# Windowed attention with an MLP-mixer block: the order of the operations written anew

## The chip, the cores and the metric

The kernel runs on one core of a Trainium2 chip. The engines named below are PE (matrix multiplication; PEld is its load of weights, which overlaps), DVE (elementwise work), ACT (elementwise work and functions such as exp and relu), POOL (here it only issues transfers, on a queue of its own) and SP (issues transfers on another queue). PSUM is the memory in which PE leaves its sums; it has 8 banks. The metric is the time of one execution in microseconds (us) on the device, the median of several runs.

## The reference

```python
scores = q @ k.T / sqrt(D) + bias          # B=8, H=8, S=576, D=64
mask = (rel >= 0) & (rel < 128)            # rel = i - j; bias = -slope[h] * |rel|
attn = exp(where(mask, scores, -1e9) - max); attn /= attn.sum(-1) + 1e-9
x = (attn @ v) with the heads side by side # [8, 576, 512]

h = relu(x.T @ w_tok1) @ w_tok2            # per batch: 512x576 @ 576x256 @ 256x576
u = x + h.T
out = u + relu(u @ w_ch1) @ w_ch2          # 576x512 @ 512x1536 @ 1536x512, f32
```

The kernel works in bfloat16 with sums in float32. It takes exp without subtracting the maximum and gets the sum of a row of attention from a column of ones beside v.

## The kernel before, in words

**Stages of a batch.** Each of the 8 batches goes through the same stages, and in time neighbouring batches are laced into one another, so that the attention of a batch fills in among the channel matmuls of the batch before.

- `load` (line 587, issue at 597): POOL fetches 128 rows of q, k or v for all heads, converted on the way.
- `transposes` (line 736): SP turns a piece of q and k by a DMA (line 744), at the start PE does it (line 755).
- `scores` (line 772): PE multiplies q and k for one block of 128 keys (line 792, 16 matmuls), ACT takes exp (line 807), DVE multiplies by the mask (line 817). `scores_two` (line 825) does two smaller ones.
- `values` (line 855): PE multiplies by v (line 872), DVE takes the reciprocals of the sums (line 902) and divides (line 905); ACT can divide too (line 910).
- `token_mix` (line 916): the two token matmuls (lines 934 and 977), relu between them (line 952), `ub` = x + h (line 995, DVE). u is then turned: by SP (line 1003) or by PE (line 1012) with a copy (line 1018).
- `unit` (line 1361) and `halves` (line 1343): the first channel matmul. In six of the batches it goes in three units each, 18 units in all, where seven products of half-size blocks take the place of eight. `halves` makes the sums of inputs (DVE, line 1355). A product is 4 matmuls on PE (line 1392) into a PSUM bank. `keep` copies a bank to a float32 buffer (ACT, line 1407, or DVE, line 1408), `join` adds a bank to such a buffer (DVE, line 1416), then relu (line 1418 or 1420).
- `second` (line 1605): the second channel matmul, also by seven products (PE, line 1669). `evict` adds a bank and u into an output buffer (DVE, line 1640) and `store` sends it out (line 1652; SP, and POOL in batches 5 and 6).
- The last 64 rows of S are done for a pair of batches at once (lines 1535 and 1580 on PE, 1587 on DVE, 1596 the store).

**Buffers.** Every kind of buffer is a ring of a fixed number of slots: 5 for q with k, 5 for v, 7 for turned q and k, 3 for exp, 6 of 128x512 float32 (`ob`; both `keep` and the output use them), 8 banks of PSUM and others. An operation that takes a slot waits for everything that still uses what was in it, transfers out of it among them.

**The order.** The program first collects 1559 operations, numbered in the order in which they are made; numbers are written in base 36. `follow` (line 132) then reads three strings:

```python
seq = [self.ops[number(x)] for x in ORDER.split()]
for x in ELSEWHERE.split():
    o = ops[number(x)]
    o.eng, o.cost, o.emit = o.other
line = {e: [o for o in seq if o.eng == e] for e in ("PE", "ACT", "DVE", "POOL", "SP")}
places = iter(PLACES)
for o in seq:
    for b in o.bufs:
        if b.slot is None:
            first = number(next(places))
```

`ORDER` holds all numbers once; each engine carries out its own operations in the order in which they stand there, one after the other, so that an operation that waits holds up all behind it on its engine. `ELSEWHERE` names the operations that run on their other engine (ACT for DVE, or DVE for ACT). `PLACES` gives, in the order of first use, the slot of each new buffer. `emit` writes the program out in the order of the planned starts. Which engine an operation waits for follows from the data and from the slots; nothing in the operations themselves depends on the strings.

**Operations that the prediction names**, all of batch 3 and the pair before it unless a batch is given:

| numbers | line | engine | what |
|---|---|---|---|
| dw, dx, dy | 1669, 1640, 1652 | PE, DVE, SP | last product of a second channel matmul, its eviction, the store |
| dm, du, dq, 97, 9j | 1652 | SP | stores of other output buffers |
| dz, e0, e1, e2 | 1580 | PE | three matmuls each of the pair's last rows |
| e3 | 1587 | DVE | the addition behind them, into an `ob` slot |
| gi, gg, gm, gk | 1012 | PE | turns of u, four small matmuls each |
| gs, gw, gz, gu | 1392 | PE | products of a unit |
| h0 | 1407 / 1408 | ACT / DVE | `keep` copy of a product, into an `ob` slot |
| j6 | 792 | PE | a block of scores |
| j5, jb, jy | 744 | SP | turns of q and k |
| sr, t2 | 792, 872 | PE | a block of scores of batch 5, and values of batch 5 |
| 30, 33 | 597 | POOL | loads of v for batch 5 (rows 0 to 127, 128 to 255) |
| 38, 37, 3d, 36 | 597 | POOL | loads of q and k for batches 6 and 7 |

Of the kernel before, what the change touches and what calls it, by code (L numbers as in the profile page):

```python
# [70 lines left out]
class Plan:  # L71
# [60 lines left out]
    def follow(self):  # L132
        def number(x):
            return int(x, 36)

        ops, seq = self.ops, [self.ops[number(x)] for x in ORDER.split()]
        assert sorted(o.n for o in seq) == list(range(len(ops)))
        for x in ELSEWHERE.split():
            o = ops[number(x)]
# [5 lines left out]
        for o in ops:  # L145
            for d in o.deps:
                succ[d].append(o)
        places = iter(PLACES)
        for o in seq:
# [134 lines left out]
    def emit(self, spin):  # L284
# [20 lines left out]
        for _, _, go in sorted(work, key=lambda w: w[:2]):  # L305
# [37 lines left out]
ORDER = ("h i 4z f j g 52 k d e 0 l 59 7 1 2 8 4v m 3 4 4x n 4w 9 4y o a 55 5 41 50 42 56 43 53 57 44 51 p 58 54 5c q "  # L343
# [45 lines left out]
ELSEWHERE = ("4w 4y 56 5m 63 6i 71 74 78 7b 83 88 8q a5 b6 b9 c1 c3 c5 c7 c9 cj ct d3 ez fb fm fo fv g7 gh gt h6 hn i0 jk "  # L389
             "kd kg lj m0 mi mn o3 o5 pa pj pk qe qj rl rq tg ts u1 vg vn wd wi xo xq yv z4 z5 10f 10k 115 11d 12o 13b 13j "  # L390
             "13k 14l 14q 15e 15r 15w")
PLACES = ("003232244671006170016710104526473452324062714260014501022433200524173120165202465372440110001732024053675420"
          "360171042072526432720541210436114220732031100742150456206221031425610041602504206145025061031240402506450223"
          "452311670240535411003123434022130102043060114030654026104631102122032427523422017541020305640072430141305303"
          "616053003220074112200332410054176020041170345022171620132114760274303704202761355326450110130100760053143531"
          "400040251014632204003247206114537242472530264130031205304206723450251006425001454210307106420052457433163102"
          "754002075110427205524235200432307526201035207114713217106024701450404360211500207226702220541062352046021000"
          "013723101045303540003364101470053317212605030540155440361105412")
UNIT_LATE = False
SECOND_LATE = False  # L400
GATE = True
# [1360 lines left out]
```

## Time and profile before

| | |
|---|---|
| median of 3 runs | 273.8 us (273.27 to 274.88) |
| the profiled execution | 274.09 us, span 272.3 us, granted clock 1.00 |
| PE / PEld busy | 262.8 us (96%) / 198.8 us (73%) |
| DVE busy | 240.2 us (88%) |
| ACT busy | 161.6 us (59%) |
| POOL busy (issuing) | 114.8 us (42%) |
| moved by DMA | 38.61 MB, mean 142 GB/s |

The span is the time from the first to the last instruction of the profiled execution; its own time lies 1.8 us above it. A group line gives line, engine, operation, output and inputs, then the count, busy time and mean duration of one, and the idle time ahead of it with what ended that. In the view by stage each engine has its busy time and, in brackets, its count of instructions in that stretch; then the granted clock of PE, the share of the DMA engines and their rate. A row of the chain is start, length, engine and line; a row of the waits says who waited for whom, the total, the count and the longest. In a timeline row the bracket at the end is the idle time just before and what released it.

### The profile page before, as it was taken

To read this page: it belongs to the slowest core of one execution; us is meant where nothing else is said; L and a number is where in the kernel's file an instruction comes from. 1 tells how busy PE (TensorE), PEld (TensorE's weight loads), DVE (VectorE), ACT (ScalarE), POOL (GpSimd) and SP (SyncE) were. 2 spreads that over 40 slices of the span, in tenths; PEclk is the share of its full clock that TensorE was granted. 3 is DMA by queue.
4 is the path that set the end of the run, shared out by engine and by line. 5 is a ranking of instruction groups with operands and counts; after the bars stand their busy time and mean duration, and the time that the engine had idled before them with its cause. 6 is when DMAs were issued, how large, how long until landed. Compare 5 with 4: busy or idle time off the path is not lost.

```text
span 272.3 us, 7636 instructions
## 1 busy us (share of the span) xinstructions
PE 262.8 (96%) x3069; PEld 198.8 (73%) x3069; DVE 240.2 (88%) x553; ACT 161.6 (59%) x314; POOL 114.8 (42%) x147
## 2 busy tenths in 40 slices
PE   7989999999999989999999999999999999999994
PEld 4767566676686667588776877688885878689883
DVE  7886699997997789999999799999999899895993
ACT  6875696335883489509883099418963199505700
POOL 8987986627093092801980181602511220013000
PEclk9999999999999999999999999999999999999999
DMA  8999999999999999999999799988997430045006
GB/s 201 179 159 181 157 195 183 152 168 123 204 186 126 220 125 161 143 141 204 149 143 178 180 162 194 109 94 212 132 128 76 116 99 4 19 80 195 0 2 193
DMA packets 160339, 38.61 MB, mean 142 GB/s; under 512 B 146544, under 2 KB 159472, under 8 KB 160304
## 3 DMA queue, kind: packets, MB, share of 16 engines
q0 software_dynamic: 109968, 19.64, 88.5%
q1 hardware_dynamic: 49104, 17.70, 36.3%
q10 hardware_dynamic: 1232, 0.79, 1.0%
q8 instruction: 24, 0.39, 0.6%
q14 instruction: 11, 0.09, 0.1%
HBM read 35.85 MB, written 9.44 MB: 166 GB/s over the span
## 4 chain that ended last, share of the span: by engine, by line
PE 79%; DMA 9%; DVE 4%; ACT 4%; issue 2%; POOL 1%; DVEq 0%; POOLq 0%; ACTq 0%
PE ps L1669 27%; PE ps L1392 17%; PE ps L1492 7%; PE ps L872 5%; PE ps L977 4%; PE ps L792 4%; PE ps L934 4%; PE ps L1535 4%; PE ps L1580 3%; DMA qk<-in_k_dram 3%; DMA v<-in_v_dram 2%; DMA W<-in_moe_w_tok_dram 2%; ACT pe L807 2%; DMA out_dram<-raw 1%; DVE r L1416 1%
## 5 line engine op out<-in xcount | busy, mean ns | idle before, releaser
L807 ACT ACTIVATE pe<-ps 128x1024 bf16<-128x1024 f32 (+1 forms) x56 | 51.9, 974 | 17.8 <-PE ps L792 17.8
L597 POOL DMA_DIRECT2D qk<-in_k_dram x35 | 30.2, 873 | 42.0 <-DMA qkT<-qk 39.8
L1669 PEld LDWEIGHTS <-r 128*128 128x128 bf16 x384 | 36.6, 98 | 7.5 <-issue 1.7
L597 POOL DMA_DIRECT2D v<-in_v_dram x36 | 31.0, 873 | 23.7 <-PE ps L872 21.7
L597 POOL DMA_DIRECT2D qk<-in_q_dram x35 | 30.2, 875 | 18.5 <-DMA qkT<-qk 15.6
L1407 ACT COPY raw<-ps 128x512 f32<-128x512 f32 x41 | 23.7, 603 | 15.2 <-PE ps L1392 14.0
L1416 DVE TENSOR_TENSOR r<-ps,raw 128x512 bf16<-128x512 f32 x46 | 30.9, 680 | 2.1 <-PE ps L1392 1.3
L1392 PE MATMUL ps<-tt,WS 128*128 128x256 bf16 x216 | 31.0, 273 | 1.4 <-DVE raw L1587 1.4
L1669 PEld LDWEIGHTS <-s 128*128 128x128 bf16 x288 | 27.6, 98 | 6.2 <-DVE s L1517 0.8
L817 DVE TENSOR_TENSOR pe<-pe,mask 128x1024 bf16<-128x1024 bf16 (+1 forms) x48 | 30.5, 646 | 1.6 <-ACT pe L807 1.4
L1392 PEld LDWEIGHTS <-WS 128*128 128x128 bf16 x288 | 26.5, 98 | 6.9 <-issue 2.4
L910 ACT ACTIVATE xb<-ps,rt 128x64 bf16<-128x64 f32 (+1 forms) x88 | 20.4, 331 | 18.4 <-DVE rt L902 18.0
L1669 PE MATMUL ps<-WC,r 128*128 128x256 bf16 x192 | 25.7, 273 | 0.0
L872 PEld LDWEIGHTS <-pe 128*128 128x128 bf16 (+1 forms) x480 | 20.2, 99 | 6.3 <-issue 1.3
L1669 PE MATMUL ps<-WT,s 128*128 128x256 bf16 x192 | 24.8, 273 | 0.0
L1669 PE MATMUL ps<-WT,r 128*128 128x256 bf16 x192 | 24.4, 273 | 0.0
L872 PE MATMUL ps<-v,pe 128*128 128x65 bf16 (+1 forms) x480 | 23.1, 194 | 0.1
L1392 PEld LDWEIGHTS <-WC 128*128 128x128 bf16 x216 | 20.0, 98 | 4.3 <-issue 0.8
L1640 DVE TENSOR_TENSOR raw<-ps,ub 128x512 f32<-128x512 f32 x28 | 19.2, 684 | 4.5 <-PE ps L1669 3.9
L1652 POOL DMA_DIRECT2D out_dram<-raw x8 | 5.7, 720 | 38.5 <-DVE raw L1640 38.1
L995 DVE TENSOR_TENSOR ub<-ps,xb 128x512 bf16<-128x512 f32 x32 | 20.9, 681 | 1.0 <-PE ps L977 1.0
L1392 PE MATMUL ps<-uT,WC 128*128 128x256 bf16 x144 | 20.7, 273 | 0.0
(146 smaller groups left out, 521.1 us busy)
## 6 DMA issues: line engine op xcount, KB each, us to landing
out_dram<-raw SPq DMA_DIRECT2D x20, 256.0 KB, 3.2
qk<-in_q_dram POOLq DMA_DIRECT2D x30, 128.0 KB, 5.3
qk<-in_k_dram POOLq DMA_DIRECT2D x30, 128.0 KB, 5.6
v<-in_v_dram POOLq DMA_DIRECT2D x28, 128.0 KB, 5.2
WC<-in_moe_w_ch_dram POOLq DMA_DIRECT2D x8, 384.0 KB, 7.4
out_dram<-raw POOLq DMA_DIRECT2D x8, 256.0 KB, 2.7
v<-in_v_dram POOLq DMA_DIRECT2D x16, 64.0 KB, 4.6
out_dram<-ob SPq DMA_DIRECT2D x4, 256.0 KB, 3.0
```

Of the source, the lines that this page charges most:

```text
L597: nc.gpsimd.dma_start(out=to()[p0 : p0 + n, :, :], in_=rows(src, b, s0, n))
L807: act_.activation(out=pb()[:, e, :, lo:, c0:c1_], in_=wide(e)[:, :, lo:, c0:c1_], func=ACT.Exp, scale=scale)
L817: dve_.tensor_tensor(out=o, in0=o, in1=heads(mk, es), op=ALU.mult)
L872: pe_.matmul(view(e)[a:z, i, :], lhsT=pb()[:, e, i, kind, a:z], rhs=vb()[:, HEADS[e][i], 0 : D + 1], start=start, stop=stop, skip_group_ch ...
L910: act_.activation(out=x4()[:, i, :], in_=view(e)[r0:r1_, i, 0:D], func=ACT.Copy, scale=rt()[r0:r1_, 0, i, :])
L995: plan.op("DVE", 690, lambda blk=blk, ht=ht, hs=hs: dve_.tensor_tensor(out=ub()[:, blk, :], in0=ht()[:, hs], in1=xb()[:, blk, :], op=ALU.a ...
L1392: pe_.matmul(bk()[:, c * HS : (c + 1) * HS], lhsT=l(c, cb), rhs=r(cb), start=new and c == 0 and cb == 0, stop=cb == 1, skip_group_check=True)
L1407: return plan.op("ACT", 600, lambda: act_.copy(out=e()[:, :], in_=bk()[:, :]), rk + UNIT_RANK, makes=e, uses=[bk], other=("DVE", 690, lamb ...
L1416: add = plan.op("DVE", 690, lambda: dve_.tensor_tensor(out=o(), in0=half_of(bk), in1=half_of(e), op=ALU.add), rk + UNIT_RANK, uses=[bk, e] ...
L1492: pe_.matmul(ct()[:, :], lhsT=WC1[:, cb, t * P : (t + 1) * P], rhs=uT()[:, cb, :], start=cb == 0, stop=cb == NCB - 1)
L1640: dve_.tensor_tensor(out=v, in0=bk().rearrange("p (c n) -> p c n", c=2), in1=src, op=ALU.add)
L1669: pe_.matmul(bk()[:, c * HN : (c + 1) * HN], lhsT=l(t, c), rhs=w(t), start=first, stop=g == 1 and t == HK - 1, skip_group_check=True)
```

## The change

`ORDER`, `ELSEWHERE` and `PLACES` are replaced. The first 129 entries of `ORDER` stay as they were, and nothing else in the file is touched: the same 1559 operations with the same data dependencies, another order on each engine, another choice of slots and banks. `ELSEWHERE` goes from 76 to 71 entries: 35 operations return to their first engine, 30 others move away from theirs. PE, SP and POOL keep their counts (555, 80, 142); ACT goes from 244 to 245, DVE from 538 to 537. The three rows of `ORDER` with the operations of the table, before and after, the whole of `ELSEWHERE` and the start of `PLACES`:

```diff
--- before.py
+++ after.py
@@ -343,59 +343,59 @@
...
-         "dt gb gd g9 gf dw j5 dz dx gi gg gj gm e0 kg gh gn gk jy dm jb du gl go e1 gq j6 gs j9 gp e2 j7 gr gw h9 gt "
-         "dy dq gz e3 gx ha h0 ja gy j8 26 29 2p gu gv jn h4 h1 jq jh h5 jo hb h2 jr jp jj hc h7 h8 hg hd hi he hh jk "
...
-         "nu 2y 3b 32 iz 35 36 sp iv sq pz q3 mz nf q1 33 nb 3a u1 q5 30 n7 n8 q7 q6 px q4 sw nc n0 nh n9 ni nl nj nk "
-         "ng nm nn np nq nr q9 nv qd sr qe qa ss qh qf qg qk qb qi st nw nx qm ql qp su qn t8 t2 sv t4 qc t5 qq qu qj "
...
-ELSEWHERE = ("4w 4y 56 5m 63 6i 71 74 78 7b 83 88 8q a5 b6 b9 c1 c3 c5 c7 c9 cj ct d3 ez fb fm fo fv g7 gh gt h6 hn i0 jk "
-             "kd kg lj m0 mi mn o3 o5 pa pj pk qe qj rl rq tg ts u1 vg vn wd wi xo xq yv z4 z5 10f 10k 115 11d 12o 13b 13j "
-             "13k 14l 14q 15e 15r 15w")
-PLACES = ("003232244671006170016710104526473452324062714260014501022433200524173120165202465372440110001732024053675420"
...
+         "fu d6 fv g1 g2 dr g3 g4 fz fw g0 g5 g6 ds 27 2a 28 do g7 4q dl dt j5 4n 29 2s 2c 2d 26 gc ge dm dp gf ga gb "
+         "g8 97 9j dq du dv dw jb gd g9 2j gm dx dz gn gk gi dy gj gl gg gh go 4r e0 gq j6 gw 4j gp gr gs j7 gt j8 e1 "
+         "gx j9 e2 gu gz e3 gv h9 h0 gy ja ha 9b jn h4 jh 2g 2h jq h5 h1 jo hb h7 hc 2m jj jr h8 h2 jp hg hd he hh hi "
...
+         "m0 ph mt nd mq mu mw ls pi pj pk mb mc sp 30 38 ps lt mx pt mr ms pu n4 mv my sw n5 pv n6 mz q2 py pw ne q3 "
+         "q7 me 37 3d 36 px na sr nt nb pz nf q0 n7 ss st nc q1 su u1 sv n1 nu 33 t2 nh n8 n0 n9 t4 md q4 q5 ni 3e 3j "
...
+ELSEWHERE = ("4w 4y 56 5m 63 6i 6u 74 7b 7m 83 86 88 a5 at b6 b9 bz c5 cf cl cr d1 el en f9 fm ft fw gj gn h0 hn i8 jk jv "
+             "kd kg lm m0 m5 o3 o5 pj pk pu rl rq tg ts ty u1 ux vn wd xo xq yv yx 10f 10k 115 11a 11d 12o 13b 13k 13v 14g "
+             "14t 159")
+PLACES = ("403222140674016170016700104526373452324062704260014501012423400107514612541720056420512131043042027522651042"
+          "007613652044203135257326220570034113040370002746354165011546311124526020421426042021003204035040225665320347"
...
```

On SP the operations around dy stand before as j4, j5, jy, dm, jb, du, dy, dq and after as j4, j5, dm, 97, 9j, dq, du, jb, dy, 9b, jy. On POOL the loads around 30 stand after as 30, 38, 37, 3d, 36, 33.

More of the change, by code (lines that the diff above doesn't have):

```diff
@@ L345 @@
          "x 6v 5u 5r y 6j 5s 46 47 66 72 6k 5v z 6a 48 6b 10 6d 6l 6g 6e 6h 6f 67 6m 6c 68 6i 11 69 6n 6p 6o 12 6s 6q "
[43 rows of a table removed]
-ELSEWHERE = ("4w 4y 56 5m 63 6i 71 74 78 7b 83 88 8q a5 b6 b9 c1 c3 c5 c7 c9 cj ct d3 ez fb fm fo fv g7 gh gt h6 hn i0 jk "
-             "kd kg lj m0 mi mn o3 o5 pa pj pk qe qj rl rq tg ts u1 vg vn wd wi xo xq yv z4 z5 10f 10k 115 11d 12o 13b 13j "
-             "13k 14l 14q 15e 15r 15w")
-PLACES = ("003232244671006170016710104526473452324062714260014501022433200524173120165202465372440110001732024053675420"
[L393 to L398, printed above, removed]
[43 rows of a table added]
+ELSEWHERE = ("4w 4y 56 5m 63 6i 6u 74 7b 7m 83 86 88 a5 at b6 b9 bz c5 cf cl cr d1 el en f9 fm ft fw gj gn h0 hn i8 jk jv "
[3 more added lines that the diff above has]
+          "007613652044203135257326220570034113040370002746354165011546311124526020421426042021003204035040225665320347"
+          "300256411702243512201540323101004320010107502744157602651020002645247315241414207451121212071462333104055231"
+          "171100345060146251130211301004353065612020557002725623107602374440172000674524310300201337300241005361211024"
+          "621325034033016206121743240105764242326240265130404012323675043030454042360520460016224100100751055136120021"
+          "740207504103720553410521413204760332451134000732410207012401634052460012502613420153070520340263420152164327"
+          "013114360320304006750642347000240565720451120053170305025631420")
 UNIT_LATE = False
```

77 rows, old and new, of the table ORDER are left out of this document.

## The prediction

> **What bounds the kernel now.** I read the page's busy shares and chain by engine first, then busy time by stage, then the chain in order of time, last the waits.
>
> ```profile
> PE 262.8 (96%) x3069; PEld 198.8 (73%) x3069; DVE 240.2 (88%) x553; ACT 161.6 (59%) x314; POOL 114.8 (42%) x147
> ...
> PE 79%; DMA 9%; DVE 4%; ACT 4%; issue 2%; POOL 1%; DVEq 0%; POOLq 0%; ACTq 0%
> ```
>
> ```profile
> core 0: us, PE busy (x) PEld busy (x) DVE busy (x) ACT busy (x) POOL busy (x), PEclk, DMA share, GB/s
> 30.00:95.00 65.00, 65.00 (x727) 44.12 (x727) 57.17 (x127) 39.67 (x78) 34.43 (x42) 1.00 1.73 171
> 95.00:113.00 18.00, 16.30 (x207) 12.03 (x206) 16.85 (x43) 16.06 (x33) 12.73 (x16) 1.00 1.56 145
> ...
> 133.00:140.00 7.00, 6.68 (x91) 4.77 (x90) 6.97 (x16) 5.55 (x12) 7.00 (x9) 1.00 2.20 142
> ...
> 140.00:160.00 20.00, 20.00 (x208) 15.22 (x209) 17.46 (x36) 8.73 (x17) 6.31 (x10) 1.00 1.43 174
> 160.00:171.00 11.00, 10.66 (x142) 8.27 (x139) 10.81 (x32) 10.72 (x22) 4.46 (x7) 1.00 1.59 165
> ...
> 219.00:231.00 12.00, 11.76 (x165) 9.51 (x164) 11.94 (x33) 11.83 (x24) 1.20 (x3) 1.00 0.15 46
> 231.00:268.50 37.50, 37.50 (x357) 31.57 (x354) 30.87 (x61) 14.25 (x29) 3.59 (x5) 1.00 0.25 69
> sum 238.50, PE 235.82 PEld 179.28 DVE 216.79 ACT 141.81 POOL 89.12; mean PE 26.20 PEld 19.92 DVE 24.09 ACT 15.76 POOL 9.90
> ```
>
> PE is the bound: from 30 to 268.5 us it is busy 235.82 of 238.50. An order can therefore give back only the 2.68 us of idling and what little is hidden in matmuls that ran slower than their pace. 1.70 of the 2.68 lies in one stage (18.00 − 16.30), 0.34 at 160–171, where DVE is full too, 0.32 at 133–140, 0.24 at 219–231. The clock is 1.00 in every stage. The chain, with start and length, and the waits name the large one:
>
> ```profile
> 89.50 0.65 PE ps L1580 x3
> 90.15 0.67 PE ps L1012 x12
> ...
> 91.94 3.98 DMA out_dram<-raw
> 96.01 0.70 DVE raw L1587
> 96.75 0.61 PE ps L1392 x4
> ...
> 124.00 0.55 PE ps L792 x16
> ...
> 162.24 1.12 DVE pe L817 x2
> ...
> 164.44 0.59 DVE r L1416
> 165.07 0.60 PE ps L1392 x4
> ...
> 248.57 6.99 PE ps L1392 x64
> ```
>
> ```profile
> DVE raw L1587 <- DMA out_dram<-raw: 1.6, 1, 1.6
> ...
> PE ps L1392 <- DVE raw L1587: 1.4, 1, 1.4
> ```
>
> ```profile
> 94.79 0.60 PE L1392 MATMUL ps<-tt,WS 128*128 128x256 bf16 x4
> 96.75 0.60 PE L1392 MATMUL ps<-tt,WS 128*128 128x256 bf16 x4 [1.36 <-DVE raw L1587]
> ```
>
> A store (operation dy) issued at 91.94 lands at 95.92. The DVE addition e3 (L1587) reuses that buffer of ob and waits 1.59 us for it; the product gu on PE waits for e3. A product of four matmuls is paced at 6.99/16 = 0.44 us, so gu was due at 94.79 + 0.44 = 95.23 and is 1.52 us late: 1.36 shown idle, 0.16 hidden.
>
> **The change, part by part.** Only the strings differ. PE runs 555 operations before and after, POOL 142, SP 80; DVE goes from 538 to 537 and ACT from 244 to 245. PE's sum of work is unchanged, so every gain or loss is a wait.
>
> *Opening and end: 0.* PE's first 39 operations, DVE's first 46 and POOL's first 24 are the same, and so are the last stores. From 231 us PE idles 0.00, and its work is fixed.
>
> *The store wait: −1.5.* Two things change. First, the next user of dy's buffer. Between dw (the matmuls behind dy) and e3, PE did dz, gi, gg, gm, e0, gk, e1, j6, gs, e2: four of 0.65 (L1580), four turns of 0.67/3 = 0.22 (L1012), a score block of 0.55 (L792), a product of 0.44, together 4.47. Now the buffer's next user is h0, a copy of a product that moves from ACT to DVE, and before it stand gm, dz, gk, gi, gg, e0, j6, gw, gs, e1, e2, gu, gz: 4×0.65 + 4×0.22 + 0.55 + 4×0.44 = 5.79. The need is 1.3 us later. Second, SP's queue:
>
> ```profile
> 85.17 4.03 SPq L744 DMA_TRANSPOSE qkT<-qk  x2
> 89.29 0.53 SPq L1652 DMA_DIRECT2D out_dram<-raw  x1
> 89.93 1.28 SPq L744 DMA_TRANSPOSE qkT<-qk  x1
> 91.30 2.18 SPq L1652 DMA_DIRECT2D out_dram<-raw  x2
> ```
>
> ```profile
> 96.01 0.69 DVE L1587 TENSOR_TENSOR raw<-ps,ub 128x512 f32<-128x512 f32 x1 [1.59 <-DMA out_dram<-raw]
> ```
>
> ```profile
> GB/s 145 144 153 156 137 222 193 41 27 10 9 10 10 47 278 280 271 206 313 380 379 220 207 257 194 46 2 9 10 197 389 383 386 382 379 389 144 0 0 1
> ...
> out_dram<-raw SPq DMA_DIRECT2D x3, 256.0 KB, 3.9
> ...
> qkT<-qk SPq DMA_TRANSPOSE x3, 4.7
> ```
>
> (The last fence is the DMA view of 85 to 97 us in 40 slices.) Before, SP issued the turns j5 and jy, then dm, the turn jb, du, dy. Now it issues j5, five stores (dm, 97, 9j, dq, du, all of data that is ready by then), jb, dy, and jy only two places later. So: j5 from 85.17 with about 1.3, five stores at 0.53 to 89.1 (0.64 each: 89.7), jb at 89.7, dy at 91.0, where it was 91.94. By its old 3.98 it lands at 95.0. The other reading is that it lands behind the turn issued before it: 89.7 + 4.7 = 94.4, and 256 KB more at about 380 GB/s, 0.7 us: 95.1. I take the later. h0 wants the buffer at 96.01 − 1.59 + 1.3 = 95.7. Spare: 0.6 us, thin. So the term is −1.52, with −0.5 as its other bound if the turn takes a microsecond and a half longer than its median here, and 0 where it is worse still. What is late next: jb's score block, which PE reaches 0.44 behind the place where gu was due, at 95.7, 1.3 after jb's landing; jy's is due some seven microseconds of PE work later.
>
> The Trainium skill, "DMA: Bandwidth & Descriptors", section "Issuing engines are not separate DMA queues", says that transfers begun by different engines end up on the same 16 DMA engines and interleave, so that spreading or bunching the issues saves only issue time. By it, issuing dy 0.9 us sooner would bring it in no sooner than the five stores ahead of it let it; their 1.28 MB at 380 GB/s are 3.4 us, so the sum stays the same as long as they end before jb.
>
> *Batch 5's score block sr and its values t2: −0.4.* They move 9.0 us of PE work ahead, out of the crowded stage 160–171 into the second products of the batch before, where PE never idles.
>
> ```profile
> 159.47 0.42 PE L872 MATMUL ps<-v,pe 128*128 128x65 bf16 x8
> 159.73 0.60 PE L1392 MATMUL ps<-uT,WC 128*128 128x256 bf16 x4
> ```
>
> ```profile
> L902 DVE RECIPROCAL rt<-ps 128x4 f32<-128x4 f32 (+1 forms) x64 | 10.5, 174 | 2.2 <-PE ps L872 1.4 <-issue 0.3
> L905 DVE TENSOR_TENSOR xb<-ps,rt 128x256 bf16<-128x256 f32 (+1 forms) x42 | 17.3, 417 | 0.6
> ```
>
> The stage loses 0.55 + (159.73 − 159.47) = 0.81 of PE work and, on DVE, two masks of 1.12 together, a reciprocal of 0.17 and a division of 0.42: 1.71. What DVE had over PE falls by 1.71 − 0.81 = 0.90. Bounds: 0 (the wait at 165.07 stays, for the join at 164.44) and −0.90. The idle shown there, 0.34, is what can surely be had: −0.4 with what hides in slow matmuls. Where they go, DVE gets the 1.71; the cover is its own free time there, 20.00 − 17.46 at 140–160. Without that cover the −0.4 would be 0.
>
> *The rest: 0, between −0.6 and +0.6.* The orders of 133–140 and 219–231 hardly change their mix, and the idle of both is 0.32 + 0.24; I leave it. In the other stages, with the groups' mean durations laid along both orders, the longest stretch by which DVE or ACT could hold PE up stays within 0.2 us of before in batches 3, 4, 6 and 7.
>
> Sum: 274.09 (span 272.3) − 1.5 − 0.4 = 272.2 for a profiled execution. The median shown is 273.8, 0.3 below the profiled one, so 271.9.
>
> **Rivals.** *The v load comes late for t2 (slower).* With t2 9.0 us ahead, its two v loads do not move by as much.
>
> ```profile
> 139.27 0.28 PE L872 MATMUL ps<-v,pe 128*128 128x65 bf16 x4
> ```
>
> ```profile
> L597 POOL DMA_DIRECT2D v<-in_v_dram x36: 686/898/1000, 7.5 to 204.1; - x36
> ...
> DMA to landing us min/median/max: 3.4/5.0/10.1
> ```
>
> t2 is due at 159.47 − 9.0 − 1.5 = 149.0. Load 30 reuses a slot that the values at 139.27 give up; by PE's new order these are 1.1 us of work sooner, and with the store wait gone 30 issues at 139.4 − 1.1 − 1.5 = 136.8. Behind it POOL has the k and q loads 38, 37, 3d, 36 (38 waits for a turn's slot) and then load 33, five issues of 0.9: 141.3, landing at the median 5.0 at 146.3, 2.7 ahead of t2. With the longest landing it is 151.4, 2.4 late, and if 38's turn is two late as well, 4.4. It decides from a lateness of 1.9, where it has eaten the gain: 274.1 − 1.9 + 4.4 = 276.6, by the median 276.3. For it: the DMA share just before is the highest, 2.20 at 133–140. Against: 2.7 us of spare.
>
> The Trainium skill, "TensorE: Matmul & The Clock Gate", section "Part 1: The HAM clock gate", says that an idle window of about 3.4 us halves PE's clock until it has been busy for as long. Here the 1.36 us of idle left the clock at 1.00, and no row has a longer one; in this rival it would add an estimated 1.7 us (3.4 us of work at half speed).
>
> *The store wait stays or moves (no change).* dy or jb lands two microseconds later than counted (turns and stores share the DMA engines with POOL's loads), h0 waits 1.4 or more and DVE's joins behind it hold up PE as e3 did, or another of the rewritten waits takes the place: 273.0 to 274.5. For it: 0.6 of spare against landings that spread from 3.4 to 10.1 us. Against: both need and issue move the right way.
>
> *All of it (more).* The 0.90 of the batch-5 stage whole and the 0.56 of the two other stages: 272.2 − 0.5 − 0.56 = 271.1, by the median 270.8. For it: DVE is full in just these stages; against: most of their idle is spread in waits of 0.2 us.
>
> **How the numbers follow.** Forecast 271.9 (its own range 271.2 to 272.9) 0.45; more, 0.12; no change, 0.28; late load, 0.15. A measurement of this kernel tells about 0.5% from no change: faster is below 272.4, slower above 275.2. Of the forecast 0.40 lies below 272.4, and with the 0.12 that is 0.52 faster; 0.33 the same, 0.15 slower. The range 270.4 to 275.0 leaves out the end of "more" and most of the late load.
>
> **What would show it.** Right: the wait of L1587 or of L1407/L1408's copies for the store is gone, PE's busy time at 95–113 is about 17.8 of 18 and the batch-5 stage has less than 0.2 idle. Wrong: a copy at L1408 waiting for a store near 95 us; PE at L872 waiting for a v load near 149; a new idle stretch over 0.5 us on PE before a scores block (a turn that came late) in batches 3 to 5.

## The result, and the profile after

The changed kernel takes 271.8 us in the median (270.97 to 275.18, 11 runs) where the kernel before takes 273.6 (272.16 to 275.06, 11 runs) in the same comparison: a ratio of 0.994, 95% interval 0.9911 to 0.9969. The ratio leaves out the one run of 275.18, which fell in the chip's slower state. Forecast were 271.9 against 273.8. The profiled execution took 272.45 us with a span of 270.6, so it lies 0.65 above the median of its kernel.

The page of the changed kernel, busy shares and chain by engine, then its view by stage (columns as in the prediction):

```profile
PE 262.0 (97%) x3069; PEld 198.6 (73%) x3069; DVE 239.8 (89%) x552; ACT 162.6 (60%) x321; POOL 114.9 (42%) x147
...
PE 77%; DMA 7%; DVE 7%; POOL 4%; ACT 3%; issue 2%; DVEq 0%; POOLq 0%; ACTq 0%
```

```profile
95.00:113.00 18.00, 17.19 (x215) 12.46 (x213) 17.83 (x45) 16.89 (x37) 12.89 (x16) 1.00 2.07 147
...
133.00:140.00 7.00, 7.00 (x97) 5.59 (x92) 6.27 (x16) 6.10 (x13) 1.83 (x3) 1.00 1.42 146
...
160.00:171.00 11.00, 10.73 (x135) 7.82 (x134) 10.45 (x29) 10.64 (x25) 8.45 (x11) 1.00 1.99 150
...
219.00:231.00 12.00, 11.66 (x155) 9.54 (x154) 11.53 (x31) 10.80 (x22) 0.00 (x0) 1.00 0.20 42
```

The stage at 95 to 113 us idles 0.81 on PE where it idled 1.70, and 133 to 140 nothing where it idled 0.32. DVE is now the full engine in the first of them: 17.83 of 18. The wait for the store is gone. SP's queue around it reads, and then on DVE the additions and copies around its buffer, e3 (L1587) and h0 (L1408), by the timelines of SP and DVE:

```profile
83.08 1.23 SPq L744 DMA_TRANSPOSE qkT<-qk  x1
84.66 1.75 SPq L1652 DMA_DIRECT2D out_dram<-raw  x3
87.48 0.37 SPq L1652 DMA_DIRECT2D out_dram<-ob  x1
87.90 0.47 SPq L1652 DMA_DIRECT2D out_dram<-raw  x1
88.48 1.27 SPq L744 DMA_TRANSPOSE qkT<-qk  x1
90.53 0.89 SPq L1652 DMA_DIRECT2D out_dram<-raw  x2
```

```profile
94.94 0.68 DVE L1587 TENSOR_TENSOR raw<-ps,ub 128x512 f32<-128x512 f32 x1
95.53 0.68 DVE L1408 COPY raw<-ps 128x512 f32<-128x512 f32 x1
```

dy is issued at 90.53 and lands 3.1 us later, at 93.62; h0 (L1408) takes its slot at 95.53 without a wait, 1.9 us later. In its place stand smaller waits, by the waits of PE and in PE's timeline:

```profile
PE ps L1392 <- DVE r L1416: 0.5, 2, 0.4
...
PE ps L872 <- DVE pe L850: 0.3, 1, 0.3
```

```profile
102.01 0.60 PE L1392 MATMUL ps<-tt,WC 128*128 128x256 bf16 x4 [0.36 <-DVE r L1416]
...
103.35 1.03 PE L1392 MATMUL ps<-uT,WC 128*128 128x256 bf16 x8 [0.19 <-DVE xb L905]
...
107.43 0.30 PE L872 MATMUL ps<-v,pe 128*128 128x65 bf16 x4 [0.27 <-DVE pe L850]
...
162.90 0.60 PE L1392 MATMUL ps<-tt,WC 128*128 128x256 bf16 x4 [0.19 <-DVE r L1416]
```

Stages shift by a microsecond or two between kernels, so windows of the clock do not compare like with like. For the experiments I therefore laid all PE operations one after the other, each at the pace at which its kind runs unhindered, and read by how much an execution is ahead of the first profile of before at the same amount of PE work done. A loss counted in this way (late by PE's pace) also holds what the idle time of a timeline leaves out. The stretches of the table are named by the clock of before; the kernels in its lower rows are those of the experiments.

| us gained on the first profile of before | to 91 | 91–97 | 97–110 | 110–133 | 133–146 | 146–160 | 160–171 | 171–end | sum |
|---|---|---|---|---|---|---|---|---|---|
| changed kernel | 0.02 | 1.52 | −0.54 | 0 | 0.68 | −0.01 | 0.31 | −0.20 | 1.78 |
| changed, second profile | 0.69 | 1.52 | −0.53 | 0 | 0.68 | −0.01 | 0.30 | −0.19 | 2.47 |
| changed, third profile | 0.25 | 1.52 | −0.42 | 0 | 0.68 | −0.11 | 0.30 | −0.12 | 2.10 |
| before, second profile | 0.39 | 1.43 | −0.05 | 0 | −0.04 | 0 | 0 | 0.05 | 1.78 |
| before, five operations elsewhere | 0.33 | 1.16 | −0.10 | 0 | 0.09 | 0 | −0.01 | −0.07 | 1.40 |
| before, SP's queue | 0.27 | 1.36 | 0 | 0 | 0.11 | 0 | −0.03 | 0.04 | 1.75 |
| before, slots | 0.02 | 1.52 | 0.01 | 0 | 0.27 | 0 | 0 | −0.18 | 1.64 |
| before, both repairs | 0.33 | 1.52 | 0.01 | −1.40 | −0.19 | 0 | 0 | −0.32 | −0.06 |

One thing stands out that the single profile had hidden: before itself, in a second execution, gains 1.43 us at 91 to 97.

### The profile page after: what moved, and what is told of

Its sections match the earlier page's. It is cut to its first block, busy times and chain, and to the rows that moved or that the text cites. A ratio compares the mean times of both kernels' runs of the same rounds, so it can differ in the third digit from the quotient of the medians.

```text
span 270.6 us, 7652 instructions
## 1 busy us (share of the span) xinstructions
PE 262.0 (97%) x3069; PEld 198.6 (73%) x3069; DVE 239.8 (89%) x552; ACT 162.6 (60%) x321; POOL 114.9 (42%) x147
## 4 chain that ended last, share of the span: by engine, by line
PE 77%; DMA 7%; DVE 7%; POOL 4%; ACT 3%; issue 2%; DVEq 0%; POOLq 0%; ACTq 0%
PE ps L1669 26%; PE ps L1392 17%; PE ps L1492 7%; PE ps L977 5%; PE ps L934 5%; PE ps L792 4%; PE ps L872 4%; PE ps L1580 4%; DMA qk<-in_k_dram 3%; PE ps L1535 3%; DMA W<-in_moe_w_tok_dram 2%; ACT pe L807 2%; DVE pe L817 2%; DMA uT<-ub 2%; POOL v L606 1%
## 5 line engine op out<-in xcount | busy, mean ns | idle before, releaser
L910 ACT ACTIVATE xb<-ps,rt 128x64 bf16<-128x64 f32 (+1 forms) x92 | 21.7, 334 | 19.0 <-DVE rt L902 18.9
L1392 PE MATMUL ps<-tt,WS 128*128 128x256 bf16 x216 | 30.9, 273 | 0.1
L1392 PEld LDWEIGHTS <-WS 128*128 128x128 bf16 x288 | 26.2, 98 | 4.8 <-DVE tt L1355 0.4
L872 PEld LDWEIGHTS <-pe 128*128 128x128 bf16 (+1 forms) x480 | 20.8, 99 | 7.2 <-issue 1.1
L1669 PE MATMUL ps<-WC,r 128*128 128x256 bf16 x192 | 25.1, 273 | 0.0
L872 PE MATMUL ps<-v,pe 128*128 128x65 bf16 (+1 forms) x480 | 23.7, 194 | 0.3 <-DVE pe L850 0.3
L1392 PEld LDWEIGHTS <-WC 128*128 128x128 bf16 x216 | 20.2, 98 | 4.3 <-issue 1.4
L1652 POOL DMA_DIRECT2D out_dram<-raw x7 | 5.0, 720 | 42.7 <-DVE raw L1640 22.1
L1392 PE MATMUL ps<-uT,WC 128*128 128x256 bf16 x144 | 20.6, 273 | 0.2 <-DVE xb L905 0.2
```

Source lines behind the costliest of these rows:

```text
L872: pe_.matmul(view(e)[a:z, i, :], lhsT=pb()[:, e, i, kind, a:z], rhs=vb()[:, HEADS[e][i], 0 : D + 1], start=start, stop=stop, skip_group_ch ...
L910: act_.activation(out=x4()[:, i, :], in_=view(e)[r0:r1_, i, 0:D], func=ACT.Copy, scale=rt()[r0:r1_, 0, i, :])
L1392: pe_.matmul(bk()[:, c * HS : (c + 1) * HS], lhsT=l(c, cb), rhs=r(cb), start=new and c == 0 and cb == 0, stop=cb == 1, skip_group_check=True)
L1669: pe_.matmul(bk()[:, c * HN : (c + 1) * HN], lhsT=l(t, c), rhs=w(t), start=first, stop=g == 1 and t == HK - 1, skip_group_check=True)
```

## The experiments

### One repair of the store wait at a time, and the share of engines at 133 to 140 us

**Another user for dy's slot.** Slots 1 and 2 of the ob ring trade places from e3 on:

```diff
 ob slots in PLACES
-e3: 1   h0: 2   hh: 2   ik: 2   lc: 1   ...
+e3: 2   h0: 1   hh: 1   ik: 1   lc: 2   ...
```

> The kernel before with one thing changed: from the addition e3 on, slots 1 and 2 of the ob ring trade places, so that e3 takes a slot that nobody holds and h0 is the next user of dy's slot. The orders and the store's time are as before (landing near 95.9). Expected: no wait of L1587 for the store; h0's copy at L1407, wanted near 95.5, waits some 0.4 us for it, little of which reaches PE. Theory 1 (the gain of the store wait stays): PE 1.3 to 1.5 us ahead of before at 97 us and as much at the end, about 272.2. Theory 2 (what follows is limited by DVE, which after the wait is busy without a break): 1.3 to 1.5 ahead at 97 us, 0.9 to 1.0 ahead from 110 us on, about 272.7.

Measured: 272.69 us against 273.38, ratio 0.9985 (0.9962 to 1.0009). e3 starts at 94.31 without a wait; the copy h0 on ACT does not wait either (timelines of DVE and ACT):

```profile
94.31 0.68 DVE L1587 TENSOR_TENSOR raw<-ps,ub 128x512 f32<-128x512 f32 x1
```

```profile
94.97 1.56 ACT L1407 COPY raw<-ps 128x512 f32<-128x512 f32 x3
```

The repair is at work in this execution: dy landed at 95.18, so in its old slot e3 would have waited nearly 1 us. In the stretch 91 to 97 PE gains 1.52 us on the first profile of before and keeps it to 110: theory 1 holds for the order of before, theory 2 falls. But the median gains 0.7 us only, and that not clear of zero.

**Only SP's queue.**

```diff
 SP in ORDER
-j5 jy dm jb du dy dq
+j5 dm dq du jb dy jy
```

> The kernel before with SP's queue alone changed around dy: j5, dm, dq, du, jb, dy, jy in place of j5, jy, dm, jb, du, dy, dq. Buffers and the other engines as before. Expected: dy issued near 90.6, landing near 93.7, before e3 wants the slot at 94.4: the wait gone by this alone. Rival: stores of ready data and the turn jb lie in the same queue, and dy lands at 95 as I had counted by the turn's landing: 0.6 of the wait left. Theory 1: then 1.5 us at the end, about 272.1; theory 2: 1.0, about 272.7.

Measured: 272.65 against 273.38, ratio 0.9988 (0.9966 to 1.001). dy was issued at 90.2 and landed at 94.28, and e3 still waited 0.2:

```profile
DVE raw L1587 <- DMA out_dram<-raw: 0.2, 1, 0.2
```

So neither expectation of the landing was right: it lies in between, 4.1 us after the issue where the changed kernel's dy takes 3.1. The gain in the median, 0.7, is as large as that of the other repair, again with zero inside its interval.

**Five operations of batch 4 on their other engine.**

```diff
 ELSEWHERE
-mi (copy, L1408), m5, lm (relu, L1418): DVE;  mn (relu), pa (division, L910): ACT
+mi, m5, lm: ACT;  mn, pa: DVE
```

> The kernel before with five operations of batch 4 near 133 to 140 us on the engine that they have in the changed kernel: the copy mi and the relus m5 and lm from DVE to ACT, the relu mn and the division pa from ACT to DVE. Order and slots as before. Theory 3 (DVE is full there, 6.97 of 7 us, and it is the share between DVE and ACT that the change repairs): the waits of PE at 137.2 and 138.5 shrink, PE is 0.4 to 0.6 ahead from 140 us on, about 273.1. Rival (it is the order of the matmuls): 0.1 or less, 273.6.

Measured: 273.25 against 273.38, ratio 0.9998 (0.9982 to 1.0015). The waits of PE at 137.2 and 138.5 (0.20 and 0.39 late by PE's pace) are gone, but a block of scores waits ahead of them for an exp on ACT, which takes over three of the five operations and gives two away. The stretch gains 0.09, no more than the 0.11 of a kernel in which no operation changes engine (SP's queue):

```profile
132.29 0.23 PE L792 MATMUL ps<-qkT 64*128 64x128 bf16 x2 [0.36 <-ACT pe L807]
```

Theory 3 falls: the share between DVE and ACT alone does not make the 0.68 of the changed kernel. By the same profile e3's wait for the store, which this edit does not touch, is 0.43 in place of 1.59:

```profile
94.51 0.69 DVE L1587 TENSOR_TENSOR raw<-ps,ub 128x512 f32<-128x512 f32 x1 [0.43 <-DMA out_dram<-raw]
```

### sr and t2 put back in the changed kernel

```diff
 ORDER (changed kernel): sr ss st su sv t2 t4 t5
-sr ... t5 among the second products of batch 4, from 145.1 us on
+sr ... t5 some 9 us of PE work later, ahead of np, ql, nx, qg, qn, qp, qq
 PLACES: bank of qh 6 -> 5, bank of t2 4 -> 3
```

> The changed kernel with the score block sr, its two exps and masks, the values t2 with reciprocal and division put back to where they stood in the order of before, some 9 us of PE work later (banks of PSUM of two operations chosen anew). Theory 4 (as predicted): the stage from 160 us loses 0.3 to 0.4 us, 272.1 to 272.2 against 271.8. Rival: nothing, since the wait for the join ahead of the product near 163 us stays 0.35 with and without the move: 271.8.

Measured: 277.53 against 273.38, ratio 1.0168 (1.013 to 1.0207). This is no fair test of theory 4, through my own choice of banks: sr's two halves take banks 4 with 5 and 6 with 7, so the product qh in bank 5 and a later one, qf, in bank 7 wait for the exps of sr, and the values t2 wait 1.60 more for an exp (PE's timeline):

```profile
154.80 0.60 PE L1392 MATMUL ps<-uT,WC 128*128 128x256 bf16 x4 [0.35 <-ACT pe L807]
...
157.85 0.60 PE L1392 MATMUL ps<-tt,WS 128*128 128x256 bf16 x4 [2.01 <-ACT pe L807]
...
162.23 0.40 PE L872 MATMUL ps<-v,pe 128*128 128x65 bf16 x8 [1.60 <-ACT pe L807]
```

It shows that order and banks go together here: sr and t2 cannot be put back with these banks. One thing in this profile speaks for the rival all the same. In the stretch from 160 us, counted as in the table, this kernel still gains 0.29 on before, with sr and t2 back in their old place, where the changed kernel gains 0.30. But the 4 us of waits just ahead gave DVE and ACT time to catch up, so it does not settle the matter.

### Both kernels profiled again, the copy h0 back on ACT, and a late v load

**Before, again.**

> The kernel before, unchanged, profiled once more. In its first profile the turn j5 started at 85.17, dy landed at 95.91 and e3 waited 1.59 us; in the profile of the kernel in which only five operations near 135 us changed engine, j5 started at 83.39 and e3 waited 0.4 us for the same store in the same order. Theory 5 (the wait depends on when POOL's loads for j5 land, and the first profile caught it at its longest): j5 between 83 and 85, the wait of L1587 for the store well under 1.59, about 0.4 to 0.8. Rival (a wait of 1.5 is the rule): 1.3 to 1.7.

Measured: the profiled execution took 272.35 us, 1.74 less than the first, and e3 waits for the store by 0.16 only:

```profile
94.18 0.69 DVE L1587 TENSOR_TENSOR raw<-ps,ub 128x512 f32<-128x512 f32 x1 [0.16 <-PE ps L1392]
```

The view puts this wait down to a product on PE, but e3 does not read that product (L1392). It starts 0.09 us behind dy's landing at 94.09, just as it starts 0.09 to 0.10 behind it in the three other profiles where it waits (95.91, 94.42 and 94.28), so the wait is for the store. The length can be followed back. In the first profile the two loads issued near 78.5, one of which j5 turns, take 6.5 us to land; in the second 4.8 (DMA views of that microsecond, first profile, then second):

```profile
qk<-in_q_dram POOLq DMA_DIRECT2D x2, 128.0 KB, 6.5
```

```profile
qk<-in_q_dram POOLq DMA_DIRECT2D x2, 128.0 KB, 4.8
```

j5 starts 0.1 behind the later landing of the two, at 85.17 and at 83.00 (0.4 of the difference is that the load was issued sooner), and the stores and turns behind it on SP move with it:

```profile
83.00 4.04 SPq L744 DMA_TRANSPOSE qkT<-qk  x2
87.14 0.53 SPq L1652 DMA_DIRECT2D out_dram<-raw  x1
87.78 1.29 SPq L744 DMA_TRANSPOSE qkT<-qk  x1
89.17 1.29 SPq L1652 DMA_DIRECT2D out_dram<-raw  x2
```

dy lands at 94.09 in place of 95.91. It could hardly have been issued sooner: the addition dx, whose result it carries out, ends at 90.06, and dy is issued at 90.08 (DVE's timeline, second profile and then first):

```profile
89.38 0.68 DVE L1640 TENSOR_TENSOR raw<-ps,ub 128x512 f32<-128x512 f32 x1
```

```profile
89.77 0.68 DVE L1640 TENSOR_TENSOR raw<-ps,ub 128x512 f32<-128x512 f32 x1
```

In the first profile dx ends at 90.45, and SP's queue holds dy back to 91.94. With SP's queue changed dx ends at 90.17 and dy is issued at 90.20, in the changed kernel at 90.50 and 90.53. So the queue costs something only in an execution in which j5 is late, and the single profile of the changed queue, with 0.2 of wait left, does not show what that repair is worth. Theory 5 holds, and more strongly than put: over three profiles of this order (first, second, and that with five operations elsewhere) e3's wait for the store is 1.59, 0.16 and 0.43. What makes the loads slower in one execution was not followed further.

**The changed kernel, again.**

> The changed kernel, unchanged, profiled once more. Its first profiled execution took 272.45 us against a median of 271.8. Theory 5: no wait of L1587 or L1408 for a store again; the waits of PE near 102 and 107 us (0.52 and 0.43 late, behind DVE's joins and masks) are there again, as they belong to the order; the stage near 133 to 140 us again loses 0.2 or less; what differs by execution lies in waits for transfers, above all ahead of 30 us. Rival: the waits near 102 and 107 are chance and gone.

Measured: 271.75 us in the profiled execution. The waits near 102 and 107 us are there again, so they belong to the order; the stretch 133 to 146 gains the same 0.68; the other difference between the two executions is 0.67 us ahead of 91 us.

```profile
101.31 0.60 PE L1392 MATMUL ps<-tt,WC 128*128 128x256 bf16 x4 [0.33 <-DVE r L1416]
...
106.76 0.30 PE L872 MATMUL ps<-v,pe 128*128 128x65 bf16 x4 [0.26 <-DVE pe L850]
```

**h0 on ACT.**

```diff
-ELSEWHERE (changed kernel): ... gj gn h0 hn i8 ...
+ELSEWHERE:                  ... gj gn hn i8 ...
```

> The changed kernel with the copy h0 (the one that takes dy's slot) back on ACT, as before; all else as in the changed kernel. DVE loses 0.6 us ahead of the joins that PE waits for at 102.0, ACT gains 0.5 ahead of an exp at 96.4. Theory 6 (the 0.55 us that the changed kernel gives back between 101 and 108 us comes from DVE being full, 17.83 of 18 us): the waits at 102 and 107 shrink to 0.5 together, PE 0.4 to 0.5 ahead of the changed kernel from 110 us, 271.4. Rival (ACT is as full, and an exp later holds up as much): 271.8 or slower.

Measured: 271.72 against 273.04, ratio 0.9958 (0.9939 to 0.9976). In the profile the stretch 97 to 110 us gives back 0.19 in place of 0.53, and DVE is off its limit:

```profile
95.00:113.00 18.00, 17.59 (x215) 12.79 (x216) 17.22 (x44) 16.73 (x38) 12.06 (x15) 1.00 2.05 175
```

Theory 6 holds for about 0.3 of the 0.5 us by the profile; in the median the kernel cannot be told from the changed one (ratio 0.994 to before).

**A late v load.** Load 33 goes behind the next three loads on POOL:

```diff
 POOL in ORDER (changed kernel)
-30 38 37 3d 36 33 3e 3j 3o
+30 38 37 3d 36 3e 3j 3o 33
```

> The changed kernel with the load 33 of v, one of the two that t2 needs, moved behind the next three loads on POOL, so that it is issued near 145.2 in place of 142.5 and lands near 150 where t2 stands at 148.65. This makes the slow rival of the prediction true in part. By that rival PE idles for what it is late, about 1.2 us (0 to 6 with the spread of landings), and the end moves by as much: about 273.0. Other way: the lateness is made up further on, where PE waits for DVE anyway near 163 us: 272.4 or less.

Measured: 273.76 against 273.04, ratio 1.0031 (0.9998 to 1.0064), some 2 us above the 271.8 that the changed kernel had in two other comparisons. The load was issued at 144.20 and landed at 149.98; t2 waits 1.98 (timeline of PE), and the end is 2.1 later than in the second profile of the changed kernel (0.36 against 2.47 ahead of the first profile of before): nothing is made up behind it.

```profile
150.12 0.40 PE L872 MATMUL ps<-v,pe 128*128 128x65 bf16 x8 [1.98 <-DMA v<-in_v_dram]
```

```profile
149.00:151.00 2.00, 0.89 (x14) 0.86 (x15) 0.51 (x2) 0.00 (x0) 0.00 (x0) 1.00 1.25 236
```

The clock stays at 1.00 through it. The Trainium skill, "TensorE: Matmul & The Clock Gate", section "Part 1: The HAM clock gate", puts the window after which the clock halves at about 3.4 us; this trace agrees as far as it goes: the longest idle stretch of PE behind the start in any profile here is 2.0 us, and none tests the figure itself.

### How much of the gain is the store

**Both repairs in the kernel before**, the slots and SP's queue together, and **the changed kernel** beside it on one chip.

> The kernel before with both repairs of the store wait, slots 1 and 2 of ob traded from e3 on and SP's queue as j5, dm, dq, du, jb, dy, jy; all else as before. No wait of e3 or h0 for a store is left in any execution. Theory 7 (the wait is 0 to 1.5 us by execution, some 0.7 in the median, and the rest of the gain is the order): 0.6 to 0.8 below the kernel before on this chip, and 0.7 to 1.1 above the changed kernel. Rival (as predicted, the store wait is most of the gain): 1.5 below before, within 0.3 of the changed kernel.

> The changed kernel, timed beside the kernel with the two repairs on the same chip. Theory 7: 1.4 to 1.8 below the kernel before, 0.7 to 1.1 below the kernel with the repairs. Rival: within 0.3 of the kernel with the repairs. Its profile is a third look at the stages: the waits behind DVE near 102 and 107 us there, the stage near 133 to 140 us with 0.2 late or less.

Measured: the repairs 272.54, the changed kernel 271.84, before 273.27; ratios 0.998 (0.9953 to 1.0007) and 0.9941 (0.9908 to 0.9975). So by the medians the repairs are worth some 0.7 us and the rest of the order another 0.7, as theory 7 had it. Neither is clear of zero: the first is not in any of the three kernels that show it (0.69, 0.73, 0.73), and for the second the two intervals overlap. The profile of the repaired kernel shows how time that was gained can be lost again further on. PE is some 1.85 us ahead at 110, with no wait for dy; then the turn of u in batch 3 is late (waits of DVE, and its timeline):

```profile
DVE tt L1355 <- DMA uT<-ub: 2.1, 2, 1.8
DVE raw L1640 <- DMA out_dram<-raw: 1.9, 1, 1.9
```

```profile
122.13 0.42 DVE L1355 TENSOR_TENSOR tt<-uT 128x512 bf16<-128x512 bf16 x1 [1.79 <-DMA uT<-ub]
```

By 124 us 1.1 of the 1.85 are lost, by 133 us 1.4. The other line, a wait of DVE for a store at 248.8 us, cost PE nothing. That execution took 274.15, the slowest of its twelve. In the second profile of before, as far ahead at that place, the turn was not late, so it is not shown that the repairs bring this wait about.

## Why the prediction was right, and where it was not

The time, 271.9 for 271.8, and its sign were right. The terms were right in part, and that they add up so well is in good part luck: −1.5 for the store and −0.4 for batch 5 were forecast, and by the medians the store is worth about −0.7 and all the rest as much again. Of the three signs that were to show the forecast right, the first came, no wait for the store; PE's busy time at 95 to 113 was 17.19 and not 17.8, and the stage of batch 5 idles 0.27 and not less than 0.2.

*PE is the bound.* Right. PE's instructions are the same 3069, and the 2 us of the late load went to the end whole.

*The store wait, −1.5.* The mechanism was right for the slot: with h0 as the next user e3 does not wait, though dy lands 0.9 behind e3's start. For SP's queue it is plausible but not shown: the queue held dy back in the first profile, by 1.49 us, but with the queue changed 0.2 of the wait was left, no less than the 0.16 in the second profile of before. The size is what failed: the step "274.09 − 1.5" took one execution's wait for the rule. It is 0.16, 0.43 and 1.59 us in three executions of the same order, long where the load that j5 turns took 6.5 us, and short where it took 4.8 and 5.0; in the median the repairs give about 0.7. The spare I feared thin, 0.6, was 1.9: dy was issued 0.5 sooner than the 91.0 I counted, as soon as dx was done, and landed 3.1 behind its issue where I had counted 4.1. The rule quoted from the Trainium skill, "DMA: Bandwidth & Descriptors", section "Issuing engines are not separate DMA queues", that transfers begun by different engines interleave on the same 16 DMA engines, is not tested by this. With SP's queue alone dy was issued as early as in the second profile of before (90.20 and 90.08) and landed no sooner (94.28 and 94.09), although two stores and a turn had changed places; but all of them were issued by one engine, SP.

*What the stage gives back.* Missed. I wrote that the other stages stay within 0.2. Between 97 and 110 us the new order loses 0.42 to 0.54 in all three profiles, by joins, masks and a division on DVE that PE waits for. Moving h0 to DVE, for which the prediction had no price on DVE, is 0.3 of it by one profile; the other 0.2 is open.

*Batch 5, −0.4.* Near in size: 0.30 to 0.31 in each profile of the changed kernel, 0.0 in all of before. The mechanism is not confirmed. The wait for the join that the lower bound of 0 rested on did stay, 0.19 idle at 162.90 (0.35 late by PE's pace, as it was at 165.07), and with it half of the 0.34 idle that "can surely be had". What went is a block of scores at 162.11 waiting for an exp (0.25 late) and values at 163.81 waiting for a division (0.24); a new wait of 0.29 for a division came at 163.74. That it is sr and t2 that do this is argued only: with both put back the stretch gained 0.29 all the same, though behind long waits.

*The rest, 0.* Failed at 133 to 146 us: 0.68, which is 0.4 to 0.9 above the other profiles of the order of before (−0.19 to 0.27) and by itself more than the bound of 0.6 that I had given for all the rest. Three waits of the first profile are gone, for a join, and for a division on ACT and one on DVE (134.16, 137.24 and 138.50 us). I had said that this stage hardly changes its mix, but five operations change engine there and the order of the matmuls is new. The engines alone gain 0.09. Whether it is the order of the matmuls was not tried by itself.

*The rivals.* The late v load did not come, though its spare was half of what I counted: 33 landed 1.2 to 1.9 us ahead of t2 in three profiles, not 2.7. (Of the loads ahead of it, 36 is one of v, not of q or k; the sum is the same.) Its price was right when it was made to come, 1 us of lateness for 1 us at the end. "The store wait stays or moves" is what one execution of the repaired kernel looks like, with the turn of u. "All of it", the whole 0.90 in batch 5, did not come.

What is left: by the stretches from 97 us on, the profiles of the changed kernel are 0.1 to 0.4 us ahead of those of the order of before (leaving out the first and the one with both repairs), and the median gives the new order 0.7, itself not clear of zero. The difference may lie in executions that no profile caught, or in the start ahead of 91 us, where the profiles of one kernel differ by 0.7; the runs don't settle it.

## What to carry to other kernels

A wait for a transfer in one profiled execution is a draw, not a price: before taking it whole, ask what set the transfer's start, how far the landings of that kind spread (here 3.4 to 10.1 us for POOL's loads of q, k and v in one execution), and profile the same kernel again. What PE lost to DVE was steadier: over a whole stretch it came back to within 0.12 us in three profiles of the changed kernel, though single waits came and went (0.19, 0.21 and none near 103 us). When a buffer's wait goes, look at what the same rewrite moved onto the full engine right behind it.

## What was not expected of the hardware

The time from issue to landing of one and the same load differed by 1.7 us between two executions (6.5 and 4.8), and through two queues and one buffer that became 1.4 us at PE. The store dy took 3.0 to 3.1 us from issue to landing in the three profiles of the changed kernel and 4.0 to 4.4 in those of the kernels with the order of before, 4.1 and 4.2 where SP's queue had been changed. In the changed kernel the store issued 0.4 us behind dy took 4.7 to 5.0; what makes the difference was not found.
